# A real Fourier mix on folded data: s with s+384, d with d+256, d with 256-d, in a fused attention and feed-forward kernel

## The chip, the cores and the metric

The kernel runs on one core of one Trainium2 chip. The metric is the device time of one execution in microseconds (us). The engines are PE (the matmul engine), DVE (VectorE), ACT (ScalarE) and POOL (GpSimd). The profile also lists, for every stretch of time, the clock that PE was granted as a share of full speed.

On one core a run is called slow when it took over 1.5% more than the fastest run of the same kernel.

## The reference, cut to what matters

```python
# q, k, v: (4 batches, 8 heads, 768, 64); x: (4, 768, 512) after the attention
attn = softmax(mask(q @ k.T / 8)) ; x = attn @ v        # mask: causal, best 3 of 12 key blocks and the own block
X = np.fft.fft(x, axis=1)                               # over s, 768 points
X = np.fft.fft(X, axis=2)                               # over d, 512 points
u = x + np.real(X)
un = (u - mean(u)) / sqrt(var(u) + 1e-6)
out = u + relu(un @ w_ch1) @ w_ch2                      # 512 -> 2048 -> 512
```

The real part of the double transform is C·x·C' - S·x·S', with cosine tables C and sine tables S over s and over d. It is symmetric: row 768-k follows from row k by a change of sign in the sine part, so the kernel computes only rows 0 to 385 in the first stage.

## The kernel before

The attention of batch b, the post-processing (Fourier mix, normalisation, first feed-forward matmul) of batch b-1 and the last matmul of batch b-2 are generators. They are run in turns, one step each, and each engine gets its instructions in that order.

```python
def gen_post(b):
    # first stage: x is the weight, 386 columns of the tables stream through
    for dt in range(NDT):                                   # 4 blocks of 128 columns of d
        for st in range(NST):                               # 6 blocks of 128 rows of s
            xs = x_b[:, st, 128 * dt:128 * (dt + 1)]
            nc.tensor.matmul(yps, xs, cs_sb[:, st, :], ...)
            nc.tensor.matmul(zps, xs, ss_sb[:, st, :], ...)
        nc.scalar.copy(out=ty, in_=yps)
        nc.scalar.activation(out=tz, in_=zps, func=AF.Copy, scale=-1.0)
        nc.vector.tensor_copy(out=tyr, in_=yps[:, KH - 2:0:-1])   # rows 384..1, reversed
        nc.vector.tensor_copy(out=tzr, in_=zps[:, KH - 2:0:-1])
        yield
    # second stage: 6 blocks of rows, 8 matmuls of 512 columns each
    for kt in range(NST):
        for dt in range(NDT):
            nc.tensor.matmul(mps, ya, cd_sb[:, dt, :], ...)
            nc.tensor.matmul(mps, za, sd_sb[:, dt, :], ...)
        nc.vector.tensor_tensor(out=u_b[:, kt, :], in0=mps, in1=x_b[:, kt, :], op=add)
        if kt % 2 == 1: yield
    ...  # bn_stats and a Newton square root on DVE, un16 = (u - mean) * rstd on DVE
    yield
    ...  # unt: PE transposes of un16, then ha, hb: the first feed-forward matmul

# in the attention: gate scores g on PE, the choice of key blocks on DVE (gsb, mx, gmp),
# transposed by PE (gt) and copied by DVE to where the score matmuls (sc) read them:
for e in range(2):
    nc.vector.tensor_copy(out=qg[e][64:64 + NB, :], in_=gt[...])

for b in range(B):
    drive([gen_attention(b), gen_post(b - 1), gen_post2(b - 2)])    # as far as they exist
drive([gen_post(3), gen_post2(2)]); drive([gen_post2(3)])
```

Of the kernel before, what the change touches and what calls it, by code (L numbers as in the profile page):

```python
# [19 lines left out]
def _consts_np():  # L20
# [3 lines left out]
    KH = 386  # L24
    s = np.arange(S)
    kk = np.arange(KH)
    arg = 2.0 * np.pi * ((np.outer(s, kk) % S) / S)
    CS = np.cos(arg).astype(np.float16)
    SS = np.sin(arg).astype(np.float16)
    d = np.arange(DM)  # L30
    argd = 2.0 * np.pi * ((np.outer(d, d) % DM) / DM)
    CD = np.cos(argd).astype(np.float16)
    SD = np.sin(argd).astype(np.float16)
# [10 lines left out]
    return dict(CS=CS, SS=SS, CD=CD, SD=SD, ident32=ident32, ident16=ident16,  # L44
# [4 lines left out]
def kernel(  # L49
# [17 lines left out]
    KH = S // 2 + 2  # L67
# [13 lines left out]

    cs_sb = cpool.tile([128, NST, KH], F16, tag="c_cs", name="cs_sb")
    ss_sb = cpool.tile([128, NST, KH], F16, tag="c_ss", name="ss_sb")
    cd_sb = cpool.tile([128, NDT, DM], F16, tag="c_cd", name="cd_sb")
    sd_sb = cpool.tile([128, NDT, DM], F16, tag="c_sd", name="sd_sb")
# [36 lines left out]
    def emit_fft_consts():  # L122
        nc.gpsimd.dma_start(cs_sb, dr["CS"].ap().rearrange("(st p) k -> p st k", p=128))
        nc.gpsimd.dma_start(ss_sb, dr["SS"].ap().rearrange("(st p) k -> p st k", p=128))
        nc.gpsimd.dma_start(cd_sb, dr["CD"].ap().rearrange("(dt p) l -> p dt l", p=128))
        nc.gpsimd.dma_start(sd_sb, dr["SD"].ap().rearrange("(dt p) l -> p dt l", p=128))

# [213 lines left out]
    def gen_post(b):  # L341
        x_b = x_tiles[b]
        u_b = bpool.tile([128, NST, DM], FP, tag="u_b", name=f"u_{b}", bufs=2)
        yT, zN, yR, zR = [], [], [], []
        for dt in range(NDT):
            yps = pst([128, KH], f"ya_{b}_{dt}")
            zps = pst([128, KH], f"za_{b}_{dt}")
            for st in range(NST):
                xs = x_b[:, st, 128 * dt:128 * (dt + 1)]
                nc.tensor.matmul(yps, xs, cs_sb[:, st, :], start=(st == 0), stop=(st == NST - 1))  # L350
                nc.tensor.matmul(zps, xs, ss_sb[:, st, :], start=(st == 0), stop=(st == NST - 1))
            ty = bpool.tile([128, KH], F16, tag="yT", name=f"yT_{b}_{dt}", bufs=4)
            tz = bpool.tile([128, KH], F16, tag="zN", name=f"zN_{b}_{dt}", bufs=4)
            tyr = bpool.tile([128, KH - 2], F16, tag="yR", name=f"yR_{b}_{dt}", bufs=4)
            tzr = bpool.tile([128, KH - 2], F16, tag="zR", name=f"zR_{b}_{dt}", bufs=4)
            nc.scalar.copy(out=ty, in_=yps)
            nc.scalar.activation(out=tz, in_=zps, func=AF.Copy, scale=-1.0)
            nc.vector.tensor_copy(out=tyr, in_=yps[:, KH - 2:0:-1])
            nc.vector.tensor_copy(out=tzr, in_=zps[:, KH - 2:0:-1])
            yT.append(ty); zN.append(tz); yR.append(tyr); zR.append(tzr)  # L360
            yield
        for kt in range(NST):
            mps = pst([128, DM], f"mx_{b}_{kt}")
            for dt in range(NDT):
                if kt <= 2:
                    ya = yT[dt][:, 128 * kt:128 * (kt + 1)]
                    za = zN[dt][:, 128 * kt:128 * (kt + 1)]
                else:
                    ya = yR[dt][:, 128 * (kt - 3):128 * (kt - 2)]
                    za = zR[dt][:, 128 * (kt - 3):128 * (kt - 2)]  # L370
                nc.tensor.matmul(mps, ya, cd_sb[:, dt, :], start=(dt == 0), stop=False)
                nc.tensor.matmul(mps, za, sd_sb[:, dt, :], start=False, stop=(dt == NDT - 1))
# [136 lines left out]
```

## Time and profile before

| | us |
|---|---|
| median of 4 runs | 451.14 (449.48 to 453.29) |
| start: until the last attention product of batch 0 | 77.7 |
| batch 1: from there to the last product of batch 1 | 81.1 |
| round of batch 2, round of batch 3 | 99.5, 99.3 |
| tail: after the last product of batch 3 | 91.9 |

The five stretches are cut at the end of the last product of each batch's x (the multiplication by the reciprocal sum on DVE, in the timeline). I use these cuts everywhere: each has its own limit, and a mean over the whole span would mix them.

These are lines of the profile's page of the kernel before: busy time and share of PE and DVE; PE's busy share in 40 slices, in tenths; the granted clock in the same slices, in tenths; and the engines' shares of the chain that ended last.

```profile
...
PE 402.2 (89%) x2806; PEld 245.3 (55%) x2806; DVE 308.3 (69%) x1059; ACT 170.0 (38%) x363; POOL 41.2 (9%) x61
...
PE   6518999898799999997899999996999999959996
...
PEclk9655558999599999999599999998699999969999
...
PE 80%; DVE 7%; DMA 6%; ACT 5%; issue 1%; SPq 1%; ACTq 0%
...
```

PE is the limit on average. The clock row shows where that hides something: in slices 2 to 6, and in one slice of each later stretch, PE ran at or near half speed.

The table of windows of the kernel before gives, for each stretch, its length, then busy time (and instructions) of PE, PE's weight loads, DVE, ACT and POOL, then granted clock, share of DMA and GB/s. The cut inside a round, at 118.9, 218.1 and 399.3, is the start of the normalisation of the batch before.

```profile
...
core 0: us, PE busy (x) PEld busy (x) DVE busy (x) ACT busy (x) POOL busy (x), PEclk, DMA share, GB/s
0.00:77.70 77.70, 57.94 (x392) 40.87 (x392) 40.96 (x198) 41.67 (x85) 27.70 (x45) 0.65 1.08 167
77.70:118.90 41.20, 34.59 (x205) 20.91 (x205) 36.60 (x145) 26.75 (x59) 0.41 (x1) 0.95 0.46 82
...
158.80:218.10 59.30, 53.78 (x308) 30.66 (x305) 41.88 (x148) 25.53 (x57) 0.18 (x1) 0.96 0.37 84
218.10:258.30 40.20, 40.01 (x393) 26.86 (x392) 34.65 (x113) 15.82 (x34) 6.39 (x8) 0.93 0.24 16
357.50:399.30 41.80, 37.91 (x186) 17.94 (x184) 19.55 (x45) 3.50 (x8) 0.00 (x0) 0.98 0.10 38
399.30:449.50 50.20, 45.20 (x248) 24.15 (x248) 24.37 (x47) 1.50 (x2) 0.00 (x0) 0.94 0.09 32
...
```

Read it line by line. The first part of batch 1 is DVE's: 36.6 of 41.2 us busy. The first part of a round is PE's (53.8 of 59.3), except for one wait. The second part of a round is PE's alone (40.0 of 40.2). The tail up to the normalisation is PE's (37.9 of 41.8). The one long wait of PE in a round, from the view of waits in the round of batch 2 (what waited, for what, us in total, times, longest), is that of the first score matmul of pair 1 for the gate copies:

```profile
...
PE sc_1_0_0_2752 L283 <- DVE qg_1_0_2299 L266: 4.3, 1, 4.3
...
```

Lines of the timeline around the end of batch 1's attention (start, duration, engine, line, instruction):

```profile
...
156.88 0.80 PE L307 MATMUL av_3_1_2081<-v_1_3_98,ptl_3_1_1881 128*128 128x65 f16 x21
157.52 0.32 PE L350 MATMUL ya_0_2124<-cs_sb,x_926 128*128 128x386 f16 x1
157.69 0.33 PE L351 MATMUL za_0_2125<-ss_sb,x_926 128*128 128x386 f16 x1
...
```

### The profile page before, as it was taken

The page shows a single profiled execution, that of the slowest core. Times are in us where ns is not written, and L with a number is a line of the kernel's source. Part 1 is how long each engine was busy: PE and PEld are TensorE (multiplying, and loading weights), DVE is VectorE, ACT ScalarE, POOL GpSimd, SP SyncE. Part 2 cuts the span into 40 slices and gives each one's busy share as a digit, 9 for nine tenths or more (in the row PEclk, how much of TensorE's full clock was granted, in tenths as well). Part 3 has the DMA queues.
Part 4 walks back from the last instruction along what each step waited for, and adds up shares of the span by engine and source line. Part 5 has one row for each costly group of instructions (what it writes and reads, how often), then busy time and mean ns, then how long its engine had stood idle before and what let it go on. Part 6 is the DMA issues. An engine that isn't in the chain of part 4 may idle for free.

```text
span 449.5 us, 7427 instructions
## 1 busy us (share of the span) xinstructions
PE 402.2 (89%) x2806; PEld 245.3 (55%) x2806; DVE 308.3 (69%) x1059; ACT 170.0 (38%) x363; POOL 41.2 (9%) x61
## 2 busy tenths in 40 slices
PE   6518999898799999997899999996999999959996
PEld 2517756555466656454566656544665654436542
DVE  0446786799988855688898855688888733477711
ACT  1607678748533343137633244045644110010000
POOL 6705112000011110000001200000000000000000
PEclk9655558999599999999599999998699999969999
DMA  9999994833022262334022264010000011000011
GB/s 164 226 226 185 196 138 26 152 70 69 3 19 19 20 103 73 79 95 94 0 19 20 20 110 115 33 39 4 1 1 2 1 47 48 23 23 1 0 71 71
DMA packets 84980, 29.30 MB, mean 65 GB/s; under 512 B 78064, under 2 KB 80336, under 8 KB 84944
## 3 DMA queue, kind: packets, MB, share of 16 engines
q0 software_dynamic: 29184, 9.73, 18.3%
q1 hardware_dynamic: 52416, 18.28, 17.3%
q10 hardware_dynamic: 3344, 0.82, 1.1%
q8 instruction: 22, 0.36, 0.3%
q14 instruction: 14, 0.11, 0.1%
HBM read 29.87 MB, written 6.29 MB: 80 GB/s over the span
## 4 chain that ended last, share of the span: by engine, by line
PE 80%; DVE 7%; DMA 6%; ACT 5%; issue 1%; SPq 1%; ACTq 0%
DMA qn_2_181<-in_q_dram 3%; DMA id_74<-c_ident 1%; DMA qn_0_99<-in_q_dram 1%; PE ch_5_5338 L441 1%; PE ch_4_5319 L441 1%; PE ch_1_5262 L441 1%; PE ch_4_4879 L441 1%; PE ch_1_4758 L441 1%; PE ch_2_3565 L441 1%; PE ch_1_2230 L441 1%; PE ch_3_5300 L441 1%; PE ch_2_5281 L441 1%; PE ch_5_4918 L441 1%; PE ch_3_4840 L441 1%; PE ch_2_4799 L441 1%
## 5 line engine op out<-in xcount | busy, mean ns | idle before, releaser
L426 PEld LDWEIGHTS <-w_sb 128*128 128x128 f16 x256 | 25.1, 98 | 25.8 <-issue 0.6
L427 PEld LDWEIGHTS <-w_sb 128*128 128x128 f16 x256 | 25.0, 98 | 6.1 <-issue 0.7
L178 POOL DMA_DIRECT2D v_0_0_91<-in_v_dram x4 | 3.4, 854 | 121.0 <-PE av_0_0_2836 L307 65.3
L130 ACT COPY unT_0_4993<-unt_0_5003 128x768 f16<-128x768 f16 x1 | 0.8, 799 | 27.2 <-PE unt_0_5003 L415 27.2
L283 PEld LDWEIGHTS <-kI_1_88 76*128 76x128 f16 x32 | 4.1, 132 | 10.6 <-issue 10.1
L283 PEld LDWEIGHTS <-kI_1_84 76*128 76x128 f16 x32 | 4.1, 131 | 9.7 <-issue 9.2
L220 PE MATMUL tp_2_0_0_302<-id_74,qn_2_181 128*128 128x128 f32 x3 | 0.9, 430 | 9.5 <-DMA qn_2_181<-in_q_dram 9.5
L109 PE MATMUL warmps<-warm_src 128*128 128x512 f16 x22 | 6.9, 486 | 1.2 <-DVE v_0_2_93 L119 1.2
L178 POOL DMA_DIRECT2D v_0_1_92<-in_v_dram x4 | 3.3, 826 | 34.3 <-PE av_1_0_1773 L307 12.3
L283 PEld LDWEIGHTS <-kI_0_87 76*128 76x128 f16 x32 | 3.5, 111 | 4.6 <-issue 2.4
L220 PE MATMUL tp_0_0_0_194<-id_74,qn_0_99 128*128 128x128 f32 x3 | 0.9, 430 | 5.6 <-DMA id_74<-c_ident 5.6
L178 POOL DMA_DIRECT2D v_0_2_93<-in_v_dram x4 | 3.3, 828 | 27.8 <-PE av_2_0_1958 L307 10.8
L415 PE MATMUL unt_0_5003<-id_75,x_3400 128*128 128x128 f16 x6 | 1.7, 288 | 4.5 <-DVE x_3400 L408 4.5
L220 PEld LDWEIGHTS tp_2_0_0_302<-id_74,qn_2_181 128*128 128x128 f32 x3 | 0.5, 213 | 9.6 <-issue 9.6
L283 PEld LDWEIGHTS <-kI_0_83 76*128 76x128 f16 x32 | 3.6, 112 | 3.8 <-issue 1.3
L109 PEld LDWEIGHTS <-warm_src 128*128 128x128 f16 x22 | 2.6, 121 | 5.0 <-issue 2.5
L415 PEld LDWEIGHTS <-x_3400 128*128 128x128 f16 x24 | 2.1, 131 | 5.7 <-DVE x_3400 L408 5.3
L226 ACT CAST qg_0_0_190<-tp_0_0_0_194 64x384 f16<-64x384 f32 x1 | 0.5, 473 | 12.4 <-DVE qT_0_0_189 L225 12.4
L225 DVE COPY qT_0_2_297<-tp_2_0_0_302 128x384 f32<-128x384 f32 x1 | 0.6, 558 | 6.6 <-PE tp_2_0_0_302 L220 6.6
L283 PEld LDWEIGHTS <-kI_2_89 76*128 76x128 f16 x32 | 3.3, 107 | 3.0 <-issue 1.8
L225 DVE COPY qT_0_0_189<-tp_0_0_0_194 128x384 f32<-128x384 f32 x1 | 0.6, 557 | 6.2 <-PE tp_0_0_0_194 L220 6.2
L283 PEld LDWEIGHTS <-kI_2_85 76*128 76x128 f16 x32 | 3.3, 104 | 2.7 <-issue 0.6
(2748 smaller groups left out, 1418.4 us busy)
## 6 DMA issues: line engine op xcount, KB each, us to landing
w_sb<-in_moe_w_ch_dram POOLq DMA_DIRECT2D x8, 256.0 KB, 9.4
w_sb<-in_moe_w_ch_dram POOLq DMA_DIRECT2D x4, 512.0 KB, 16.7
out_dram<-u_943 SPq DMA_DIRECT2D x6, 256.0 KB, 2.4
out_dram<-u_2123 SPq DMA_DIRECT2D x6, 256.0 KB, 2.0
out_dram<-u_3417 SPq DMA_DIRECT2D x6, 256.0 KB, 2.0
out_dram<-u_4694 SPq DMA_DIRECT2D x6, 256.0 KB, 2.0
cs_sb<-c_CS POOLq DMA_DIRECT2D x1, 579.0 KB, 7.5
ss_sb<-c_SS POOLq DMA_DIRECT2D x1, 579.0 KB, 8.8
```

Of the source, the lines that this page charges most:

```text
L109: nc.tensor.matmul(wps, wsrc[:, 0:128], wsrc, start=True, stop=True)
L130: eng.copy(out=dst, in_=src)
L178: nc.gpsimd.dma_start(out=v16_t[e][sl][:, :, 0:64], in_=v[b, h].rearrange("(jt p) d -> p jt d", p=128))
L220: nc.tensor.transpose(ps[:, i, :], src[:, st, :, :].rearrange("p h d -> p (h d)"), id32)
L225: nc.vector.tensor_copy(out=qt[:, cols], in_=flat)
L226: nc.scalar.copy(out=qg[0][0:64, cols], in_=flat[0:64])
L283: nc.tensor.matmul(sp[:, co:co + (a1 - a0)], kI[e][0:76, 128 * jt:128 * (jt + 1)], qg[e][0:76, a0:a1], start=True, stop=True)
L415: nc.tensor.transpose(tps[:, st, :], un16[:, st, 128 * dt:128 * (dt + 1)], id16)
L426: nc.tensor.matmul(ha, w1s, unT[dt][:, 0:512], start=(dt == 0), stop=(dt == NDT - 1))
L427: nc.tensor.matmul(hb, w1s, unT[dt][:, 512:768], start=(dt == 0), stop=(dt == NDT - 1))
L441: nc.tensor.matmul(cps, hT[it][:, 128 * st:128 * (st + 1)], w2_sb[:, it, :], start=(it == 0), stop=(it == NIT - 1))
```

## The change

The intent is to give PE less to do. Cosines and sines of even and odd rows k are symmetric about s = 384, so the data can be added or subtracted once and each parity needs half of the rows. The same holds for d about 256, and a second time with d against 256-d. What remains are four groups of 128 columns, each of which needs either a cosine or a sine table. All folding is done on DVE.

```diff
@@ -341,37 +351,67 @@   (constants and table loads cut: 2.2 MB of tables become 1.0 MB)
     def gen_post(b):
-        for dt in range(NDT):
-            for st in range(NST):
-                xs = x_b[:, st, 128 * dt:128 * (dt + 1)]
-                nc.tensor.matmul(yps, xs, cs_sb[:, st, :], start=(st == 0), stop=(st == NST - 1))
-                nc.tensor.matmul(zps, xs, ss_sb[:, st, :], start=(st == 0), stop=(st == NST - 1))
-            ... two copies on ACT, two reversed copies on DVE
+        tt(sd[:, 0], x_b[:, 0:3, :], x_b[:, 3:6, :], ADD)
+        tt(sd[:, 1], x_b[:, 0:3, :], x_b[:, 3:6, :], SUB)
+        sf = sd.rearrange("p a t d -> p (a t) d")
+        tt(zw[:, :, 0:256], sf[:, :, 0:256], sf[:, :, 256:512], ADD)
+        tt(zw[:, :, 256:512], sf[:, :, 0:256], sf[:, :, 256:512], SUB)
+        yield
+        tt(fg[:, :, 1:128], zw[:, :, 1:128], zw[:, :, 255:128:-1], ADD)
+        tt(fg[:, :, 129:256], zw[:, :, 1:128], zw[:, :, 255:128:-1], SUB)
+        tt(fg[:, :, 257:384], zw[:, :, 257:384], zw[:, :, 511:384:-1], SUB)
+        tt(fg[:, :, 384:511], zw[:, :, 257:384], zw[:, :, 511:384:-1], ADD)
+        ... three small copies and a memset for the columns without a partner
+        yield
+        for g in range(4):
+            for par in range(2):
+                for st in range(3):
+                    nc.tensor.matmul(out_p, fg[:, 3 * par + st, 128 * g:128 * (g + 1)],
+                                     fs_sb[:, g % 2, par, st, 0:KQ], ...)       # 193 columns
+                    ... for g == 1: three matmuls with one weight column (d = 128)
+            nc.scalar.copy(out=ty (even and odd interleaved), in_=yps)
+            _copy(nc.scalar if g < 2 else nc.vector, tr (interleaved), yps reversed)
+            if g % 2 == 1: yield
         for kt in range(NST):
-            for dt in range(NDT):
-                nc.tensor.matmul(mps, ya, cd_sb[:, dt, :], ...)
-                nc.tensor.matmul(mps, za, sd_sb[:, dt, :], ...)
+            for par in range(2):
+                nc.tensor.matmul(mps[:, par, :], src[2 * par][:, rows], fd_sb[:, 3 * par, :], ...)
+                nc.tensor.matmul(mps[:, par, :], src[2 * par + 1][:, rows],
+                                 fd_sb[:, 3 * par + 1 + sg, :], ...)            # 256 columns
-            nc.vector.tensor_tensor(out=u_b[:, kt, :], in0=mps, in1=x_b[:, kt, :], op=add)
+            nc.vector.tensor_tensor(out=u_b[:, kt, :] with step 2, in0=mps, in1=x_b with step 2, op=ADD)
```

More of the change, by code (lines that the diff above doesn't have):

```diff
@@ L23, in _consts_np, with ang @@
     NB = 12
-    KH = 386
     s = np.arange(S)
-    kk = np.arange(KH)
-    arg = 2.0 * np.pi * ((np.outer(s, kk) % S) / S)
-    CS = np.cos(arg).astype(np.float16)
-    SS = np.sin(arg).astype(np.float16)
-    d = np.arange(DM)
-    argd = 2.0 * np.pi * ((np.outer(d, d) % DM) / DM)
-    CD = np.cos(argd).astype(np.float16)
-    SD = np.sin(argd).astype(np.float16)
+    p = np.arange(128)
+    KE = 194
+    fs = np.zeros((128, 2, 2, 3, KE), dtype=np.float64)
+    for par in range(2):
+        kk = 2 * np.arange(KE - 1) + par
+        for st in range(3):
+            arg = 2.0 * np.pi * ((np.outer(128 * st + p, kk) % S) / S)
+            fs[:, 0, par, st, 0:KE - 1] = np.cos(arg)
+            fs[:, 1, par, st, 0:KE - 1] = np.sin(arg)
+    m = np.arange(256)
+    le, lo = 2 * m, 2 * m + 1
+    def ang(d, l):
+        return 2.0 * np.pi * ((np.outer(d, l) % DM) / DM)
+    se = np.sin(ang(p, le))
+    se_m, se_p = -se, se.copy()
+    se_m[0] = se_p[0] = np.cos(np.pi * m)
+    so = np.sin(ang(p + 1, lo))
+    fd = np.stack([np.cos(ang(p, le)), se_m, se_p, np.cos(ang(p, lo)), -so, so], axis=1)
+    FS = fs.astype(np.float16)
+    FD = fd.astype(np.float16)
     ident32 = np.eye(128, dtype=np.float32)
@@ L43, in _consts_np @@
     IndR = (nn[:, None] == (s[None, :] // 64)).astype(np.float16)
-    return dict(CS=CS, SS=SS, CD=CD, SD=SD, ident32=ident32, ident16=ident16,
+    return dict(FS=FS, FD=FD, ident32=ident32, ident16=ident16,
                 ltri=ltri, ut01=ut01, cz24=cz24, own01=own01, IndR=IndR)
@@ L66 @@
     NIT = DF // 128
-    KH = S // 2 + 2
+    KE = 194
+    KQ = KE - 1
     NP = H // 2
@@ L80, in pst @@
         return psump.tile(shape, dtype, tag=tag, name=name, bufs=bufs)
-    cs_sb = cpool.tile([128, NST, KH], F16, tag="c_cs", name="cs_sb")
-    ss_sb = cpool.tile([128, NST, KH], F16, tag="c_ss", name="ss_sb")
-    cd_sb = cpool.tile([128, NDT, DM], F16, tag="c_cd", name="cd_sb")
-    sd_sb = cpool.tile([128, NDT, DM], F16, tag="c_sd", name="sd_sb")
+    fs_sb = cpool.tile([128, 2, 2, 3, KE], F16, tag="c_fs", name="fs_sb")
+    fd_sb = cpool.tile([128, 6, 256], F16, tag="c_fd", name="fd_sb")
     id32 = cpool.tile([128, 128], FP, tag="c_id32", name="id32")
@@ L122, in emit_fft_consts @@
     def emit_fft_consts():
-        nc.gpsimd.dma_start(cs_sb, dr["CS"].ap().rearrange("(st p) k -> p st k", p=128))
-        nc.gpsimd.dma_start(ss_sb, dr["SS"].ap().rearrange("(st p) k -> p st k", p=128))
-        nc.gpsimd.dma_start(cd_sb, dr["CD"].ap().rearrange("(dt p) l -> p dt l", p=128))
-        nc.gpsimd.dma_start(sd_sb, dr["SD"].ap().rearrange("(dt p) l -> p dt l", p=128))
+        nc.gpsimd.dma_start(fs_sb, dr["FS"].ap())
+        nc.gpsimd.dma_start(fd_sb, dr["FD"].ap())
     def _copy(eng, dst, src):
@@ L343, in gen_post @@
         u_b = bpool.tile([128, NST, DM], FP, tag="u_b", name=f"u_{b}", bufs=2)
-        yT, zN, yR, zR = [], [], [], []
-        for dt in range(NDT):
-            yps = pst([128, KH], f"ya_{b}_{dt}")
-            zps = pst([128, KH], f"za_{b}_{dt}")
-            for st in range(NST):
-                xs = x_b[:, st, 128 * dt:128 * (dt + 1)]
-                nc.tensor.matmul(yps, xs, cs_sb[:, st, :], start=(st == 0), stop=(st == NST - 1))
-                nc.tensor.matmul(zps, xs, ss_sb[:, st, :], start=(st == 0), stop=(st == NST - 1))
-            ty = bpool.tile([128, KH], F16, tag="yT", name=f"yT_{b}_{dt}", bufs=4)
-            tz = bpool.tile([128, KH], F16, tag="zN", name=f"zN_{b}_{dt}", bufs=4)
-            tyr = bpool.tile([128, KH - 2], F16, tag="yR", name=f"yR_{b}_{dt}", bufs=4)
-            tzr = bpool.tile([128, KH - 2], F16, tag="zR", name=f"zR_{b}_{dt}", bufs=4)
-            nc.scalar.copy(out=ty, in_=yps)
-            nc.scalar.activation(out=tz, in_=zps, func=AF.Copy, scale=-1.0)
-            nc.vector.tensor_copy(out=tyr, in_=yps[:, KH - 2:0:-1])
-            nc.vector.tensor_copy(out=tzr, in_=zps[:, KH - 2:0:-1])
-            yT.append(ty); zN.append(tz); yR.append(tyr); zR.append(tzr)
-            yield
@@ L362, in gen_post @@
-        for kt in range(NST):
-            mps = pst([128, DM], f"mx_{b}_{kt}")
-            for dt in range(NDT):
-                if kt <= 2:
-                    ya = yT[dt][:, 128 * kt:128 * (kt + 1)]
-                    za = zN[dt][:, 128 * kt:128 * (kt + 1)]
-                else:
-                    ya = yR[dt][:, 128 * (kt - 3):128 * (kt - 2)]
-                    za = zR[dt][:, 128 * (kt - 3):128 * (kt - 2)]
-                nc.tensor.matmul(mps, ya, cd_sb[:, dt, :], start=(dt == 0), stop=False)
-                nc.tensor.matmul(mps, za, sd_sb[:, dt, :], start=False, stop=(dt == NDT - 1))
-            nc.vector.tensor_tensor(out=u_b[:, kt, :], in0=mps, in1=x_b[:, kt, :],
-                                    op=mybir.AluOpType.add)
+        ADD, SUB = mybir.AluOpType.add, mybir.AluOpType.subtract
@@ new lines, in gen_post, with tt @@
+        sd = bpool.tile([128, 2, 3, DM], F16, tag="fold_s", name=f"sd_{b}")
+        zw = bpool.tile([128, NST, DM], F16, tag="fold_d", name=f"zw_{b}")
+        def tt(out, in0, in1, op):
+            nc.vector.tensor_tensor(out=out, in0=in0, in1=in1, op=op)
+        tt(sd[:, 0], x_b[:, 0:3, :], x_b[:, 3:6, :], ADD)
[3 more added lines that the diff above has]
+        tt(zw[:, :, 256:512], sf[:, :, 0:256], sf[:, :, 256:512], SUB)
@@ new lines, in gen_post @@
+        yield
+        fg = bpool.tile([128, NST, DM], F16, tag="fold_s", name=f"fg_{b}")
+        nc.vector.memset(fg[:, :, 128:129], 0.0)
+        tt(fg[:, :, 1:128], zw[:, :, 1:128], zw[:, :, 255:128:-1], ADD)
+        tt(fg[:, :, 129:256], zw[:, :, 1:128], zw[:, :, 255:128:-1], SUB)
+        nc.vector.tensor_copy(out=fg[:, :, 0:512:256], in_=zw[:, :, 0:512:256])
+        tt(fg[:, :, 257:384], zw[:, :, 257:384], zw[:, :, 511:384:-1], SUB)
+        tt(fg[:, :, 384:511], zw[:, :, 257:384], zw[:, :, 511:384:-1], ADD)
@@ new lines, in gen_post @@
+        nc.vector.tensor_copy(out=fg[:, :, 511:512], in_=zw[:, :, 384:385])
+        yield
+        yg, yr = [], []
+        OD = 200
+        for g in range(4):
+            yps = pst([128, 2 * OD], f"yp_{b}_{g}")
+            for par in range(2):
+                out_p = yps[:, OD * par:OD * par + KQ]
+                for st in range(3):
+                    nc.tensor.matmul(out_p, fg[:, 3 * par + st, 128 * g:128 * (g + 1)],
+                                     fs_sb[:, g % 2, par, st, 0:KQ], start=(st == 0),
+                                     stop=(st == 2))
+                    if g == 1 and st == 0:
+                        for s2 in range(3):
+                            nc.tensor.matmul(yps[0:1, OD * par:OD * par + KQ],
+                                             zw[:, 3 * par + s2, 128:129],
+                                             fs_sb[:, 0, par, s2, 0:KQ], start=False,
+                                             stop=False, skip_group_check=True)
+            ty = bpool.tile([128, 2 * KQ], F16, tag=f"yg{g}", name=f"yg_{b}_{g}")
+            tr = bpool.tile([128, S // 2], F16, tag=f"yr{g}", name=f"yr_{b}_{g}")
+            nc.scalar.copy(out=ty.rearrange("p (m two) -> p two m", two=2),
+                           in_=yps.rearrange("p (a c) -> p a c", a=2)[:, :, 0:KQ])
+            _copy(nc.scalar if g < 2 else nc.vector,
+                  tr.rearrange("p (m two) -> p two m", two=2),
+                  yps[:, 0:2 * OD - 2].rearrange("p (a c) -> p a c", a=2)[:, :, KQ - 1:0:-1])
+            yg.append(ty)
+            yr.append(tr)
+            if g % 2 == 1:
+                yield
@@ new lines, in gen_post @@
+        for kt in range(NST):
+            mps = pst([128, 2, 256], f"mx_{b}_{kt}")
+            src, sg = (yg, 0) if kt < 3 else (yr, 1)
+            rows = slice(128 * (kt % 3), 128 * (kt % 3 + 1))
+            for par in range(2):
+                nc.tensor.matmul(mps[:, par, :], src[2 * par][:, rows], fd_sb[:, 3 * par, :],
+                                 start=True, stop=False)
+                nc.tensor.matmul(mps[:, par, :], src[2 * par + 1][:, rows],
+                                 fd_sb[:, 3 * par + 1 + sg, :], start=False, stop=True)
+            nc.vector.tensor_tensor(
+                out=u_b[:, kt, :].rearrange("p (m two) -> p two m", two=2), in0=mps,
+                in1=x_b[:, kt, :].rearrange("p (m two) -> p two m", two=2), op=ADD)
```

## The prediction

> **What bounds the kernel.** Page: PE busy 89%, DVE 69%, ACT 38%; the chain that ended last is 80% PE, 7% DVE. By the timeline the work is: batch 1's attention (77 to 158 us), two equal rounds of 99.3 us (batches 2, 3, with the post-processing of the batch before), then a tail without attention (358 to 449.5). The table of windows: the tail (358 to 396: PE 37.4 of 38) and the second part of each round (217 to 258: PE 40.8 of 41) are PE-bound. The first part of batch 1 (77 to 119: PE 35.4, DVE 37.4 of 42) is DVE-bound. The first part of a round (158 to 217: PE 53.5, DVE 41.6 of 59) is PE-bound until PE waits 4.3 us for DVE (waits view, qg_1_0).
>
> **What the change removes.** Timeline: a 386-column Fourier matmul starts every 163.5 ns, a 512-column one every 216. Per batch 48 x 0.1635 + 48 x 0.216 = 18.2 us of PE. After, by columns: 30 of 193 (82 ns) and 24 of 256 (108 ns) = 5.1 us: 13.1 us less per batch, 52 in all. DVE loses 8 reversed copies of 128x384 (0.47 us apart) and gets 2 back: -2.8 us.
>
> **What it adds.** All folding is on DVE, ahead of any Fourier matmul. The mask multiply 128x128 f16 repeats every 0.135 us[...]. About 5.8 us (to 7.4), net +3 to +4.6 per batch. The six additions into u now write f32 with a step of two: 0.61 us each before[...].
>
> **How much is on the path.**
> - Tail: PE-bound, 13.1 less; the folds hide behind two blocks of the last matmul (6.9 us). The closing DVE chain grows by 0.7 to 1.5: -10.5.
> - Rounds of batches 2 and 3: PE has two blocks and transposes (8.2 us) before the first folded matmul, DVE delivers at about 11: 2.5 us wait. PE then runs ahead until the scores, where ACT (exp every 0.48 us) and DVE set the pace: -8 each.
> - Batch 1: nothing for PE during folds (6 to 8 us idle), and DVE was the limit already: +2 (-2 to +5).
> - Fourier tables shrink from 2.2 to 1.0 MB but load after the DMA wait at the start: 0.
>
> Sum -24.5: about 428 us, range 418 to 441. Chances: faster 0.93, same 0.06, slower 0.01.
>
> **What would show it.** PE busy falls by about 50 us, to 78 to 84% of the span; DVE busy rises by 12 to 25 us. Rounds of about 91 us. The first folded matmul of each batch waits for a DVE fold. Batch 1 stays near 84 us with PE idle. Folds near 0.9 and 0.5 us.
>
> **What would make it wrong.** Lower: the folds hide, rounds save 11 or more (about 415). Higher: strided f32 additions at 1.2 us, [...]folded evictions (stride 2, reversed) slower, or idle PE lowering the granted clock in batch 1 (already 0.81 to 0.86 in windows where PE waits for DVE).

The sum of the folds, 5.8 us (to 7.4) a batch, stays as my estimate, and so do the folds near 0.9 and 0.5 us; the trace has only 0.135 us from start to start for a mask multiply of 128 columns. The 2.5 us of wait in the rounds and the 6 to 8 us without work in batch 1 rest on it too. The +12 to +25 us for DVE are four times +3 to +4.6, and at the upper end an allowance for the additions. All terms of the sum in us stand: -10.5 (tail), -8 and -8 (rounds), +2 (batch 1), 0 (start) make -24.5. The 1.2 us among the reasons is twice the plain additions' 0.61 us. The clock of 0.81 to 0.86 is a mean over windows of 27 to 36 us around PE's waits, such as 200 to 227 us (0.81) and 200 to 236 us (0.86) in the kernel before.

## More of the kernel before

```profile
...
158.18 0.56 DVE L314 TENSOR_TENSOR x_926<-av_3_1_2081,rcp_3_1_2103 128x384 f16<-128x384 f32 x1
...
```

The last product of x starts at 158.18 on DVE, but the first Fourier matmul starts at 157.52. It reads only the first 128 columns of x, which are two heads that were finished long ago. The unfolded first stage hides the latency of the last heads.

## The result, and the profile after

| us | before | after | difference | predicted |
|---|---|---|---|---|
| median of 4 runs | 451.14 | 430.48 (428.18 to 430.97) | -20.7 | -24.5 |
| start | 77.7 | 82.9 | +5.2 | 0 |
| batch 1 | 81.1 | 84.8 | +3.7 | +2 |
| round of batch 2 | 99.5 | 90.9 | -8.6 | -8 |
| round of batch 3 | 99.3 | 91.0 | -8.3 | -8 |
| tail | 91.9 | 79.6 | -12.3 | -10.5 |

The ratio is 0.9542 (0.9496 to 0.9587). A ratio is the mean time of one kernel's fast runs over that of the other's of the same rounds, so it is not quite the ratio of the medians.

The same lines of the page, after:

```profile
...
PE 359.6 (84%) x2638; PEld 229.9 (54%) x2638; DVE 313.2 (73%) x1079; ACT 169.7 (40%) x355; POOL 39.1 (9%) x59
...
PE   6518999667659999998599998999599999959996
...
PEclk9655555768957999999969999999789999989999
...
PE 67%; DVE 20%; DMA 7%; ACT 4%; issue 2%; SPq 0%; ACTq 0%
...
```

PE lost 42.6 us of busy time and 13 points of the chain; DVE gained 4.9 us of busy time, but its share of the chain went from 7% to 20%. The clock row has more low digits at the start (slices 2 to 7, where before it was 2 to 6).

The table of windows after (columns as before):

```profile
...
0.00:82.90 82.90, 59.90 (x386) 42.65 (x386) 41.63 (x199) 43.73 (x88) 25.58 (x43) 0.61 0.97 146
82.90:127.60 44.70, 26.87 (x170) 18.26 (x170) 38.70 (x154) 26.96 (x58) 0.44 (x1) 0.77 0.36 67
...
167.70:219.00 51.30, 43.00 (x271) 26.37 (x268) 43.18 (x155) 26.61 (x57) 0.23 (x1) 0.94 0.42 97
219.00:258.60 39.60, 38.78 (x386) 25.98 (x386) 34.13 (x111) 14.43 (x32) 6.30 (x8) 0.95 0.24 16
349.60:379.50 29.90, 25.21 (x146) 13.31 (x143) 20.46 (x49) 3.20 (x6) 0.00 (x0) 1.00 0.14 53
379.50:429.20 49.70, 44.68 (x248) 23.97 (x248) 24.39 (x47) 1.50 (x2) 0.00 (x0) 0.95 0.09 32
...
```

In batch 1 (82.90) PE is busy for 26.9 of 44.7 us: it had time before, and has more now. In the first part of a round (167.70) PE fell from 53.8 to 43.0 us while DVE grew from 41.9 to 43.2: the two are even now, and the stretch shrank by 8.0, not by the 10.8 that PE lost. The second part of a round did not move. The tail shrank where the Fourier matmuls are (41.8 to 29.9).

PE's timeline after, at the end of batch 0's attention, and DVE's:

```profile
...
81.74 0.55 PE L230 MATMUL tp_0_1_1_981<-id_72,kn_0_924 128*128 128x128 f32 x3
89.94 1.16 PE L383 MATMUL yp_0_997<-fs_sb,fg_989 128*128 128x193 f16 x6 [7.65 <-DVE fg_989 L371]
...
93.23 0.52 PE L230 MATMUL tp_1_0_0_1038<-id_72,qn_1_929 128*128 128x128 f32 x3
...
```

```profile
...
82.37 0.56 DVE L324 TENSOR_TENSOR x_178<-av_3_1_895,rcp_3_1_917 128x384 f16<-128x384 f32 x1
82.96 1.83 DVE L359 TENSOR_TENSOR sd_940<-x_178 128x1536 f16<-128x1536 f16 x2
84.71 0.54 DVE L242 TENSOR_REDUCE kr_1_0_957<-tp_0_1_0_973 64x6 f32<-64x384 f32 x1
85.17 1.81 DVE L359 TENSOR_TENSOR zw_941<-sd_940 128x1536 f16<-128x1536 f16 x2
...
88.76 0.55 DVE L359 TENSOR_TENSOR fg_989<-zw_941 128x762 f16<-128x762 f16 x1
...
89.77 1.03 DVE L359 TENSOR_TENSOR fg_989<-zw_941 128x762 f16<-128x762 f16 x2
...
93.79 0.56 DVE L235 COPY qT_1_1_1033<-tp_1_0_0_1038 128x384 f32<-128x384 f32 x1 [2.91 <-PE tp_1_0_0_1038 L230]
...
```

After the transposes of pair 0 PE has nothing until the folds are done: 7.65 us. The folds took about what was forecast: two of 1536 columns in 1.83 us, so 0.87 us apart, and those of 762 columns, half of whose operands are read backwards, 0.47 us apart (89.22 after 88.76). The last line is the second half of the cost. The transposes of pair 1 stand behind the first Fourier matmuls in PE's order, so when DVE is done with folding it waits 2.9 us for them.

In the round of batch 2 the view of waits of PE lists, after (its four longest):

```profile
...
PE sc_1_0_0_2652 L293 <- DVE qg_1_0_2223 L276: 4.2, 1, 4.2
PE ch_5_2445 L481 <- DVE kr_2_2_2362 L242: 0.8, 1, 0.8
PE ch_1_2148 L481 <- DVE u_939 L483: 0.7, 1, 0.7
PE yp_0_2167 L383 <- DVE fg_2140 L371: 0.7, 1, 0.7
...
```

The fold costs PE 0.7 us directly and 0.7 for a matmul whose output buffer waits for an addition behind the folds. The wait for the gate copies of pair 1 is as long as before.

### The profile page after: what moved, and what is told of

Its sections match the earlier page's. It is cut to its first block, busy times and chain, and to the rows that moved or that the text cites. A ratio compares the mean times of both kernels' runs of the same rounds, so it can differ in the third digit from the quotient of the medians.

```text
span 429.2 us, 7093 instructions
## 1 busy us (share of the span) xinstructions
PE 359.6 (84%) x2638; PEld 229.9 (54%) x2638; DVE 313.2 (73%) x1079; ACT 169.7 (40%) x355; POOL 39.1 (9%) x59
## 4 chain that ended last, share of the span: by engine, by line
PE 67%; DVE 20%; DMA 7%; ACT 4%; issue 2%; SPq 0%; ACTq 0%
DMA qn_2_179<-in_q_dram 4%; DMA qn_1_137<-in_q_dram 2%; PE ch_5_3691 L481 1%; PE ch_5_2445 L481 1%; PE ch_5_5142 L481 1%; PE ch_5_4730 L481 1%; PE ch_4_4699 L481 1%; PE ch_3_5104 L481 1%; PE ch_2_5085 L481 1%; PE ch_0_5047 L481 1%; PE ch_3_4668 L481 1%; PE ch_2_4627 L481 1%; PE ch_0_4553 L481 1%; PE ch_4_3586 L481 1%; PE ch_3_3555 L481 1%
## 5 line engine op out<-in xcount | busy, mean ns | idle before, releaser
L293 PEld LDWEIGHTS <-kI_1_82 76*128 76x128 f16 x32 | 4.2, 134 | 14.3 <-issue 5.3
L293 PEld LDWEIGHTS <-kI_1_86 76*128 76x128 f16 x32 | 4.1, 130 | 8.6 <-issue 6.3
L383 PE MATMUL yp_0_997<-fs_sb,fg_989 128*128 128x193 f16 x6 | 1.2, 364 | 7.7 <-DVE fg_989 L371 7.7
L383 PEld LDWEIGHTS <-fg_989 128*128 128x128 f16 x24 | 2.4, 117 | 8.7 <-DVE fg_989 L371 7.9
L188 POOL DMA_DIRECT2D v_0_1_90<-in_v_dram x4 | 3.3, 826 | 34.6 <-PE av_1_0_1721 L317 12.4
L188 POOL DMA_DIRECT2D v_0_2_91<-in_v_dram x4 | 3.3, 828 | 28.7 <-PE av_2_0_3152 L317 10.8
L239 ACT CAST kI_2_83<-tp_2_1_0_314 64x384 f16<-64x384 f32 x1 | 0.5, 472 | 13.0 <-PE tp_2_1_0_314 L230 13.0
L236 ACT CAST qg_0_0_188<-tp_0_0_0_192 64x384 f16<-64x384 f32 x1 | 0.5, 472 | 12.7 <-DMA kn_1_138<-in_k_dram 12.7
L455 PEld LDWEIGHTS <-x_3300 128*128 128x128 f16 x24 | 2.1, 130 | 6.3 <-DVE x_3300 L448 5.8
L239 ACT CAST kI_0_81<-tp_0_1_0_2124 64x384 f16<-64x384 f32 x1 | 0.5, 472 | 12.0 <-PE tp_0_1_0_2124 L230 12.0
```

Of the source, the lines that this page charges most:

```text
L188: nc.gpsimd.dma_start(out=v16_t[e][sl][:, :, 0:64], in_=v[b, h].rearrange("(jt p) d -> p jt d", p=128))
L239: nc.scalar.copy(out=kI[0][0:64, cols], in_=flat[0:64])
L293: nc.tensor.matmul(sp[:, co:co + (a1 - a0)], kI[e][0:76, 128 * jt:128 * (jt + 1)], qg[e][0:76, a0:a1], start=True, stop=True)
L383: nc.tensor.matmul(out_p, fg[:, 3 * par + st, 128 * g:128 * (g + 1)], fs_sb[:, g % 2, par, st, 0:KQ], start=(st == 0), stop=(st == 2))
L455: nc.tensor.transpose(tps[:, st, :], un16[:, st, 128 * dt:128 * (dt + 1)], id16)
```

## The experiments

Each experiment starts from the changed kernel unless said otherwise. Runs of one set shared a chip and the runs of the kernel before; its medians were 451.16, 450.50, 449.83 and 448.57 in the four sets.

| run | median (range) | ratio to before | start | batch 1 | rounds | tail |
|---|---|---|---|---|---|---|
| e1_nofold | 417.21 (412.14 to 417.66) | 0.9245 | 79.5 | 76.7 | 89.4, 89.3 | 80.9 |
| e2_deadfold | 422.29 (421.12 to 424.26) | 0.9398 | 76.7 | 80.9 | 90.0, 90.5 | 81.3 |
| e3_act | 424.48 (423.67 to 426.22) | 0.9437 | 81.2 | 81.6 | 88.9, 88.8 | 81.4 |
| e4_hybrid | 420.47 (415.05 to 423.98) | 0.9249 | 77.3 | 80.6 | 91.1, 91.4 | 81.5 |
| e8_again | 429.84 (422.10 to 430.20) | none | 81.2 | 85.2 | 91.1, 90.5 | 80.3 |
| e5_warm | 429.77 (422.26 to 431.86) | 0.9443 | 74.3 | 84.7 | 90.9, 91.0 | 79.6 |
| e6_sonly | 450.94 (449.94 to 455.96) | 1.0047 | 76.5 | 84.7 | 99.2, 99.0 | 89.9 |
| e7_donly | 431.67 (429.37 to 433.02) | 0.9581 | 78.8 | 84.9 | 91.1, 91.5 | 83.5 |
| e9_fill | 428.39 (421.24 to 430.84) | none | 81.7 | 83.6 | 91.0, 90.4 | 79.6 |
| e10_late | 427.19 (424.73 to 430.62) | 0.9522 | 76.8 | 85.0 | 92.3, 90.6 | 80.4 |
| e11_all | 420.45 (418.79 to 421.41) | 0.9359 | 82.5 | 81.0 | 87.5, 86.4 | 79.6 |
| e12_best | 418.40 (417.14 to 418.79) | 0.9336 | 85.0 | 78.5 | 86.5, 87.5 | 79.5 |

The stretches are those of the one profiled execution of each. Where the ratio is "none", only one of the six runs counted as fast, some 7 us below the others; it was not the profiled one. The programs of after, e8 and e9 are the same until the end of batch 1, and batch 1 took 84.8, 85.2 and 83.6 us in them: differences of under 2 us between two profiles of batch 1 show nothing.

### What do the folds cost where they stand? e1_nofold, e2_deadfold

My theory was that batch 1 is longer because of DVE: it must do the folds on top of its other work, and PE waits for them. To part the two, one kernel has no folds and one does them without anybody waiting. Their outputs are wrong, which doesn't matter for the times. The Fourier matmuls read a constant tile, tied to x by a copy of one column.

```diff
 e1:  -  all folds (sd, zw, fg)
      +  nc.vector.tensor_copy(out=fg_c[:, :, 0:1], in_=x_b[:, :, 511:512])
      -  nc.tensor.matmul(out_p, fg[:, ...], ...)
      +  nc.tensor.matmul(out_p, fg_c[:, ...], ...)
 e2:  the same, but the folds stay and write tiles that no matmul reads
```

Both also fill the constant tiles once on DVE at the start, give two small tiles of the statistics four buffers and read the first warm-up matmuls from another tile. These side changes were not tested alone.

> Wrong result on purpose: the changed kernel without its folds; the Fourier matmuls read constant tiles, and only a copy of 6 elements waits for the attention output. It measures what the folds cost in all. Theory (the folds cost what PE waits for them and what they take of DVE in batch 1): the attention of batch 1 goes from 84.8 us to about 79, each round from 90.9 to about 89, the tail stays near 79.7 since PE never waits for a fold there; in all about 420 us against 430.5. Rival (the rest of the lost gain is not the folds' at all): at most 2 us less, 428 or more.

> Wrong result on purpose: all folds are done on DVE in their places, but nobody reads them; the matmuls read constant tiles as in the kernel without folds. It keeps the DVE work and takes away PE's wait. If the wait alone is the cost: as fast as the kernel without folds (about 420). If the DVE work alone is: as the changed kernel (430). I expect between: in batch 1 DVE idles 2.9 + 1.3 us after the folds waiting for PE, which goes away, so batch 1 about 81 us; each round 1.3 us less (the two waits of 0.67 us); about 424 in all.

The table of windows, from the last product of batch 0 to the normalisation, first e1, then e2 (the stretch after: 44.7 us, DVE 38.7):

```profile
...
79.50:116.30 36.80, 24.66 (x170) 16.38 (x170) 33.49 (x143) 26.87 (x58) 0.38 (x1) 0.85 0.43 81
...
```

```profile
...
76.70:118.30 41.60, 28.78 (x170) 19.86 (x170) 38.82 (x155) 26.97 (x58) 0.40 (x1) 0.73 0.38 72
...
```

Without waiting (e2) the stretch is 3.1 us shorter at the same DVE time (38.8 us): DVE's idle time fell from 6.0 to 2.8. Without the folds as well (e1) it is another 4.8 shorter, with 5.3 us less of DVE. Batch 1 as a whole: 84.8 with both, 80.9 without the wait, 76.7 without the folds. So the fold costs batch 1 some 8 us, about half as a wait and half as DVE time, and the change's +3.7 is what remains after its savings. In the rounds the folds cost 1.6 us (91.0 against 89.3); without the wait alone (e2) they took 90.0 and 90.5, 0.5 to 0.9 us less where I had expected 1.3. In the tail they cost nothing: e1 and e2 are no shorter there.

### Is it DVE that paces the rounds now? e3_act

```diff
-            _copy(nc.scalar if g < 2 else nc.vector, tr, yps reversed)
+            _copy(nc.scalar, tr, yps reversed)
-                nc.vector.tensor_copy(out=qg[e][64:64 + NB, :], in_=gt...)
+                nc.scalar.copy(out=qg[e][64:64 + NB, :], in_=gt...)
```

> Right result. Takes other work off DVE: the two reversed evictions that DVE still had, and the gate copies into the query tiles (8 of 0.47 us per batch), go to ACT, 4.7 us of DVE per batch. Theory (DVE sets the pace from the folds to the normalisation in batch 1 and before the scores of head pair 1 in each round): batch 1 about 81 us, rounds about 88, about 421 in all. Rival (ACT is as full as DVE in those places, or only latency counts): within 2 us of 430, or slower.

Correct result; rounds 88.9 (-2.1), batch 1 81.6 (-3.2), total 424.48 (expected 421). From the view of waits of PE in e3's round of batch 2:

```profile
...
PE sc L293 <- ACT qg L276: 3.1, 2, 2.9
...
```

The wait of the scores of pair 1 fell from 4.2 to 2.9 us. PE's work did not change, so in the first part of batch 1 and of each round it is DVE's queue that sets the pace after the change. The tail came out 1.8 longer than in the profile after; see the clock below.

### Fold only where PE is the limit: e4_hybrid

Batch 0's Fourier stage, which runs beside the attention of batch 1, is left as before; the others are folded. The new tables are loaded over the old ones once batch 0 is through.

```diff
+        if b == 0:
+            ... the Fourier stage as before
+        else:
             ... the folded Fourier stage
```

> Right result. Batch 0 is transformed as in the kernel before (its tables, no folds), batches 1 to 3 as in the changed one. Theory (in batch 1's attention the change costs 3.7 us, 84.8 against 81.1): batch 1 back to about 81 us, rounds and tail as in the changed kernel, 426 to 427 in all. Rival (the slower batch 1 comes from the chance of the clock or of the start, not from folding): 430, unchanged.

Correct result. Batch 1 took 80.6 us, as in the kernel before (81.1), and the rounds are those of the change (91.1, 91.4): that part was as expected. The total, 420.47, gained more than expected because the start was 77.3 and not 82.9. Its ratio of 0.9249 rests on the two of four runs that count as fast (415.05 and 417.38), so the median is the better number.

### Was the start an effect of the change? e8_again

This is the changed kernel once more.

> The changed kernel once more, unchanged, as the measure for the other three runs of this set. The start (up to the last attention product of batch 0) took 82.9 us in the profile of the change, 77.7 in that of the kernel before, though it runs the same instructions. If that is chance (when the first loads land and when the granted clock leaves 0.5), this run's start may lie anywhere between 76 and 83 and its time between 424 and 431. If the changed table loads cause it, the start is again above 82 and the time again 429 to 431. Segments otherwise as before: batch 1 84 to 85, rounds 91, tail 79 to 82.

Five of six runs took 429.5 to 430.2 us and one took 422.1; the profiled one had a start of 81.2. That decides between neither of the two theories. In the five profiles of kernels whose start has the same compute instructions as the change's (after, e5, e8, e9, e10), it took 74.3 to 82.9 us. The page's clock row of e5, with a start of 74.3, against the row after shown above:

```profile
...
PEclk9656699889969999999789999999599999989999
...
```

In e5 the clock left 0.5 for good at about 54 us, in the profile after at about 79. The range of the kernel before (445 to 453 us over all sets) is as wide. One start of 82.9 against one of 77.7 is therefore no proof. But the times of all runs say more. If what follows the start is taken to be as long in every run of a kernel as in its profile, each run's time gives an estimate of its start: 71 to 80 us, median 76, for the 44 runs of the kernel before, and 80 to 83 us for nine of the ten runs of the changed one (73 for the tenth). By this estimate a start some 5 us longer is typical of the changed kernel, and not the chance of one profile. Its cause is open: before the folds the two programs differ only in the tables and tiles and their loads, and e10, with the same start as the change, has 75 to 81 us by the same estimate.

### Is batch 1 long because idle PE loses its clock? e5_warm

The rival to the DVE theory: PE idles 7.65 us, its clock falls (in the profile after, to 0.50 from 86.5 to 93.3 us), and it then runs at half speed. The granted clock of the whole stretch was 0.77 after and 0.95 before.

```diff
+        if b == 0: warm(24, "a")        # before the first folded matmul; 512 columns, nobody reads them
+            if b == 1 and hp == 1: warm(16, "b")   # after the gate transposes of pair 1
+        if b == 0: warm(8, "c")         # before the transposes of the normalised batch
```

> Correct result. 48 matmuls of 512 columns that nobody reads, put where PE idles in batch 1: 24 before the first folded matmul, 16 after the gate transposes of pair 1, 8 before the transposes of the normalised batch 0. If batch 1 is long because idle PE loses granted clock, the clock of batch 1 stays near 1 and batch 1 falls by 2 to 4 us. If it is long because DVE has the folds to do on top of its other work, and because PE waits for them, batch 1 stays at 84 to 86 us (or grows, where the matmuls stand in the way). My theory is the second: total within 1% of the changed kernel of the same set.

The windows from the last product to the normalisation, e5 and then e8 of the same set:

```profile
...
74.30:118.90 44.60, 35.40 (x217) 22.03 (x214) 38.55 (x152) 26.94 (x58) 0.42 (x1) 0.92 0.37 67
...
```

```profile
...
81.20:127.30 46.10, 29.38 (x170) 20.26 (x170) 38.92 (x154) 27.01 (x58) 0.47 (x1) 0.71 0.35 65
...
```

The clock rose from 0.71 to 0.92 and DVE's time stayed at 38.6 and 38.9 us. Batch 1 stayed at 84.7 (85.2 in e8), though the clock records of the traces have 13.7 us at half clock in it, and 30.7 in e8. So for the stretch as a whole the rival falls. One place was not cleared: from 81.1 to 84.5 us the clock was 0.50 in e5 too, over the first 18 folded matmuls, and DVE waited 2.85 us for the transposes behind them (2.91 after). These 18 take 3.3 us there and 1.9 at full clock in a round, so an estimated 1.4 us of that wait belong to the half clock.

### Which fold pays? e6_sonly, e7_donly

```diff
 e6:  fold s with s+384 only: 48 matmuls of 193 columns, second stage as before
 e7:  fold d only: 24 matmuls of 386 columns and 6 with one weight column, second stage as in the change
```

> Correct result. Only s is folded with s+384: the first stage has 48 matmuls of 193 columns (86 ns each measured: 4.1 us, before 7.85), the second stage stays at 48 of 512 columns (10.4 us). PE loses 3.7 us a batch, DVE gets 2 folds of 0.87 us and keeps 8 reversed copies. Expected: rounds about -3 each against the kernel before, tail -3.5, batch 1 +1 to +2: 441 to 444 us. If the s fold were the better half of the change, 435 or less.

> Correct result. Only d is folded: the first stage has 24 matmuls of 386 columns (163.5 ns: 3.9 us) and 6 with one weight column (about 1 us), the second stage as in the change (24 of 256 columns, 2.6 us): about 7.5 us a batch of PE where the full change has 5.6 and the kernel before 18.2. DVE does 1.74 us less of folding, and the first Fourier matmul is ready that much sooner. Theory: what the s fold saves PE, PE waits for: same time as the full change within 1%, with batch 1 shorter by 1.5 to 2.5 us and the tail longer by 1.5 to 2. Rival: PE work is what counts, then it is 1.9 us a batch slower, 7 us in all.

I was wrong on e6. It saves PE 3.7 us a batch by the same arithmetic, and the rounds stayed at 99.1 (before 99.4). PE's timeline of e6 at the end of batch 1's attention shows where half of it went:

```profile
...
158.67 1.44 PE L311 MATMUL av<-v,ptl 128*128 128x65 f16 x42
162.22 0.26 PE L369 MATMUL ya<-fs_sb,sd 128*128 128x193 f16 x1 [2.11 <-DVE sd L352]
```

The fold needs the last head, so the first Fourier matmul waits 2.1 us where the kernel before started at once. I had not charged that. The other 1.3 us (3.7 - 2.1 - 0.3) was lost in small waits that I did not trace one by one. The tail gained 2.0 where I had expected 3.5, and batch 1 lost 3.6.

On e7 the total fits (431.67 against 429.84 for e8, under 0.5%), and so do the rounds (91.1 and 91.5 against 91.1 and 90.5). The tail is 3.2 longer than in e8, but it had 10.2 us at half clock and e8 6.8; against e3 and e4, with 10.2 too, it is 2.0 to 2.1 longer, about as expected. Batch 1 did not become shorter as I expected (84.9 against 85.2): PE waits 5.9 us for the fold there and not 7.7, but its Fourier work is longer by an estimated 1.9 us (7.5 against 5.6), about as much. So the fold of d brings nearly all of the gain. The fold of s, on top of it, is worth something only in the tail.

### Does the half clock after the waits cost anything? e9_fill

In the profiles before and after, the granted clock falls to 0.50 in the waits for the gate copies in the rounds (at 213.4 and 312.4 us before, at 212.7 and 304.9 after) and in the wait before the last transposes (at 397.7 and 380.0). It stays there for 10.2 us in the rounds and for 6.8 and 3.4 us in the tail, with PE busy for 3.0 to 9.0 us of each stretch. That looks like a second cost.

```diff
+            if b >= 2 and hp == 1: warm(17, f"b{b}")   # 3.7 us, after the gate transposes of pair 1
+        if b == B - 1: warm(22, "c")                   # 4.8 us, before the last transposes
```

> Correct result. The changed kernel with matmuls that nobody reads in PE's two long waits outside batch 1: 17 of 512 columns (3.7 us) after the gate transposes of pair 1 in the rounds of batches 2 and 3 (PE waits 4.2 us there for DVE), 22 (4.8 us) before the transposes of the last normalised batch (wait 5.3 us). In all profiles so far the granted clock falls to 0.50 in these waits and stays there for 3 to 13 us of busy PE afterwards. If the half clock is a cost of its own, beside the wait, the clock stays at 1.00 there, rounds fall from 91 to 87 to 89 and the tail by 1 to 3 us: 5 to 9 us in all. If scores there are paced by ACT and DVE and not by PE, the rounds stay at 91 and only the tail gains.

Windows around the two waits, in the round of batch 2 and in the tail, first e9, then the profile after:

```profile
...
210.00:226.00 16.00, 13.96 (x116) 9.01 (x113) 13.88 (x54) 7.06 (x14) 1.64 (x2) 0.79 0.20 13
...
376.00:390.00 14.00, 12.35 (x85) 7.12 (x84) 10.63 (x24) 1.50 (x2) 0.00 (x0) 1.00 0.01 2
...
```

```profile
...
212.00:228.00 16.00, 12.33 (x104) 7.96 (x104) 14.01 (x54) 7.50 (x15) 1.64 (x2) 0.68 0.21 15
...
379.00:393.00 14.00, 12.35 (x82) 7.78 (x83) 10.59 (x24) 1.50 (x2) 0.00 (x0) 0.88 0.00 1
...
```

In the tail the clock was 1.00 and not 0.88, and the tail took 79.6 us, as in the profile after (79.6) and in e5 (79.6); e8 had 80.3. In the round of batch 2 the clock rose only from 0.68 to 0.79, because it fell a few us later, and the rounds stayed at 91.0 and 90.4. In the round of batch 3 the clock records have 3.4 us at half clock, where after and e8 have 10.2 (91.0 and 90.5). DVE was busy for 13.9 of the 16 us either way. So as far as the clock was held there, the half clock costs nothing that could be measured, and the second theory was the right one. In the tail I had expected 1 to 3 us; what the profiles show is less. The tails of 81.3 to 81.5 (e2, e3, e4) had 10.2 us at half clock around this wait, e8 and e10 (80.3, 80.4) 6.8, the profile after and e5 (79.6) 3.4, e9 none. So the half clock costs the tail up to 2 us, by chance, and the profile after was a lucky one.

### Is it the order in PE's queue that lengthens batch 1? e10_late

```diff
         yield
+        if b == 0:
+            yield
+            yield
         yg, yr = [], []                 # the Fourier matmuls of batch 0 come two steps later
```

> Correct result. The changed kernel with the Fourier matmuls of batch 0 two steps later in the program, behind the transposes of pairs 1 and 2 of batch 1, nothing else moved. The folds on DVE stay where they are. If batch 1 is long because everything behind the first folded matmul in PE's order (the transposes of pair 1, and so DVE's next work) waits with it, batch 1 falls from 85 to 81 to 82, as in the run where the folds ran but nobody waited for them (80.9). If it is the volume of the folds on DVE, it stays at 84 to 85. Rounds and tail unchanged. The first theory is mine.

My theory fell: batch 1 took 85.0 us. PE no longer waited for a fold, but DVE's idle time was not less. DVE's waits in e10 between the last product and the normalisation:

```profile
...
DVE kr L242 <- ACT kI L240: 2.1, 2, 1.2
DVE gsb L254 <- PE g L251: 2.0, 1, 2.0
DVE qT L235 <- PE tp L230: 1.8, 1, 1.8
...
```

The wait moved: DVE now waits for the gate matmuls, the transposes and ACT's copies. The normalisation came at 52.0 us and not 44.7, with more of the attention done by then. Why e2, where nothing waits either, gains 3.9 us and e10 nothing is not settled. What differs is when the Fourier matmuls run, early in e2 and late in e10, and also the clock: the records have 41.0 us at half clock in batch 1 of e10 and 27.3 in that of e2. The round of batch 2 took 92.3, though nothing had moved there; I did not trace that.

### All together: e11_all, e12_best

e11 is e3, e9 and e10 together (14 matmuls in the rounds). e12 is e4, e3 and e9 together, and has 30 more unread matmuls in PE's wait for the loads of pair 2 at the start.

```diff
 e12: +            if b == 0 and hp == 2:
      +                warm(30, "s")
```

> Correct result. All that helped or should help, together: evictions and gate copies on ACT, the Fourier matmuls of batch 0 two steps later, matmuls that nobody reads in the waits (14 in the rounds, 22 in the tail). If the gains add: rounds 86 to 87 (91 less 2.1 for ACT, less 2 to 3 for the clock), batch 1 78 to 80, tail 78 to 79: 412 to 415 us where the changed kernel takes 430. If ACT and clock gain the same wait, 417 to 420.

> Correct result. The version that keeps what paid: batch 0 unfolded as before, batches 1 to 3 folded, evictions and gate copies on ACT, matmuls that nobody reads in the waits of the rounds (14) and the tail (22), and 30 more in PE's wait of 8 to 11 us for the loads of pair 2 at the start. Without the last, the sum of the segments of the runs behind it is 80 (start) + 79 to 80.6 (batch 1) + 2 x 87 + 80 = 413 to 415. If the start is set by the granted clock (0.50 from 22 us until 54 to 79 us in the profiles), the 30 matmuls bring it to 1.00 by about 34 us and the start to 70 to 75: 406 to 411. If the clock falls again in the attention of batch 0 anyway, the start stays at 75 to 83 and the time at 412 to 418.

Both are correct and both beat the two kernels. e11 took 420.45, just above both expectations, with a start of 82.5. Its rounds were 87.5 and 86.4, against 88.9 and 88.8 in e3: with the copies on ACT, holding the clock is worth another 1.4 to 2.4 us, which it was not in e9. (e9 held it only in part, so this comparison is not clean.) PE is close to being the limit again: busy for 42.8 of the first 44.5 us of a round, 1.7 of them with matmuls that nobody reads, where in e3 it was 38.9. e12 took 418.40, ratio 0.9336 (0.9293 to 0.9379), where the change itself had 0.9542 in its own set. It had the shortest batch 1 of the correct kernels (78.5), but the start did not shrink: with 85.0 it is the longest of all profiles. e4, whose start has neither the 30 matmuls nor the gate copies on ACT, had 77.3; which of the two lengthens it, if not the clock, was not tested. Windows of e12:

```profile
...
24.00:34.00 10.00, 7.05 (x28) 2.94 (x27) 3.07 (x21) 0.00 (x0) 2.12 (x4) 0.84 1.15 242
34.00:80.00 46.00, 41.85 (x280) 30.05 (x280) 24.79 (x125) 36.25 (x67) 9.15 (x13) 0.50 0.87 128
...
```

With the 30 matmuls the clock went up (0.84 in the ten microseconds around them), but it fell in the wait of 2.95 us behind them and stayed at 0.50 from 34 to 80 us, with PE busy for 41.9 of those 46 us. The third case of the expectation came true in kind; start and time lie just above its ranges.

## Why the prediction was right or wrong

- **The total.** 428 predicted, 430.48 measured, inside the range; faster by over 2%, as given with 0.93. The sum missed by 3.8 us, and that is less than the one term that was not in it, the start. Part of the closeness is luck: without the start the stretches sum to -25.5, and there +1.7 in batch 1 stands against -2.7 in rounds and tail.
- **The rounds: right, in size and mechanism.** -8 each predicted, -8.6 and -8.3 measured. The wait at the fold was over-sized (2.5 us predicted, 0.7 and 0.7 measured; DVE delivered 8.6 us after the last product, not 11). Of 12.6 us less of PE (18.2 before; after, 5.6 by the spacing in the trace: about 86 ns for 193 columns with 128 weight columns or one, some 180 at each of the four changes between the two kinds, and 110 for 256), 8.4 came out. The rest is 1.6 for the folds (e1) and 2.6 that is left over; I put that to DVE's pace, since moving copies to ACT returns 2.1 (e3), but it was not measured apart.
- **The tail: right, but mis-sized.** -10.5 predicted, -12.3 measured. The terms as I wrote them (13.1 less PE, 0.7 to 1.5 more at the end of DVE's chain) sum to -11.6 to -12.4; I rounded them down without a reason. The wait before the last transposes grew from 4.5 to 5.3 us, as the low end said. In five other profiles with the full change in the tail and no filling (e3, e4, e5, e8, e10) it was 79.6 to 81.5, so some of -12.3 is luck with the clock: the kernel before had 6.8 us at half clock around the wait, and with the same 6.8 the change (e8, e10) took 80.3 and 80.4, 11.5 less.
- **Batch 1: right sign, mis-sized.** +2 (-2 to +5) predicted, +3.7 measured. The two costs were named (idle PE, DVE at its limit) but not summed: by e1 and e2 they are 3.9 for the wait and 4.2 for DVE's time. The wait also blocks what stands behind it in PE's queue, and then DVE waits in turn; the prediction did not have that.
- **The start: wrong, 0 predicted, +5.2 measured.** The step that failed is the assumption that equal instructions take equal time there. The profiled starts of equal programs spread over 8.6 us (74.3 to 82.9), with the moment at which the clock leaves 0.5. By the estimate under e8 a start some 5 us longer is typical of the changed kernel; what brings it was not found.
- **DVE busy: wrong.** +12 to +25 predicted, +4.9 measured. The terms were about right: the 32 folds are busy for 22.8 us and their small copies for 1.5 (charged: 4 x 5.8 = 23.2), the copies that went took 13.3 (charged: 11.2), and the additions with a step of two, for which the upper end had an allowance, take 0.68 to 0.69 us, where the plain ones took 0.66 to 0.69. That sums to about +11. What failed is the step from terms to busy time: the view counts the overlap of neighbours once (the durations in the traces sum to 360.3 us before and 373.2 after, the busy times to 308.3 and 313.2), and instructions that the change left alone, such as the mask multiplies (mean 220 ns before and after), add an estimated 6 us less because they stand closer together. (After minus e1 gives only 18.9, because e1 has 3.6 us of DVE work of its own for its constant tile.)
- **PE busy: -50 predicted, -42.6 measured; 84% of the span, at the edge of 78 to 84.** PE's time at half clock counts as busy, and there was more of it: by the traces' clock records PE was busy at half clock for 71 us before and 87 after. Matmuls of 65 columns start every 55 ns at 0.50 and every 29 at 1.00, so half of these 16 us is about the missing 8 (an estimate).
- **The rates held.** The folds took 0.87 us (1536 columns) and 0.47 us (762 columns, one operand read backwards), near the 0.9 and 0.5 of the forecast. With the mask multiply's 0.135 us (128 columns) these three points lie on one line to about 1%: 0.53 ns per column plus some 70 ns. The f32 additions with a step of two took 678 to 693 ns where the plain ones took 659 to 692.

## What to carry to other kernels

Work taken from the busiest engine is worth its full time only where that engine is the limit; here the same 12.6 us were worth 12 in the tail, 8.4 in the rounds and less than nothing in batch 1, so cost a change stage by stage and apply it only where it pays. Ask what a new step needs before it can start: a fold in one instruction needs all of its input, and the code that it replaces may have started on a part. Idle PE and a low clock beside a long stretch are no proof of a cost; fill the idle time and see.

## What the traces show of the clock and of changing weights

- **The clock falls in PE's waits.** Each wait of 4.2 to 5.3 us in the rounds and the tail, before and after, had a fall to 0.50 in it, 2.3 us (before, at 397.7) to 5.2 us (after, at 380.0) after PE's last matmul. The stretches at 0.50 lasted 3.4 us (tail, after), 6.8 (tail, before) and 10.2 (all four rounds).
- **When it comes back is not explained.** At the start it stayed at 0.50 from 34 to 80 us in e12, with PE busy for 41.9 of these 46 us. It left 0.5 for the rest of the start at about 54 us in e5 and at 79.6 in the profile after, two kernels with the same compute instructions until then.
- **The matmuls agree with the record.** Those of 65 columns start every 55 ns at 0.50 and every 29 at 1.00, before and after (medians).
- **What it cost depends on the place.** The tail of e4 had 10.2 us at half clock and was 1.9 us longer than that of e9, which had none. In the rounds, filling the wait took away 3.4 and 6.8 us of half clock and saved at most 0.6 us (91.0 and 90.4, after 90.9 and 91.0).
- **A change of weights cost time.** In the rounds and the tail after, at clock 1.00, each of the four changes a batch between weights of 128 columns and of one took 176 to 181 ns from start to start, with 193 columns streamed. A matmul after one of its own kind took about 86. In batch 1, at clock 0.50, the four changes took 298 to 301 ns each.
